# Attention with a gMLP behind it: a fixed order in steps of two score tiles, and q and k transposed by DMA

## The chip, the cores and the metric

The kernel runs on one core of one Trainium2 chip. The metric is the device time of one launch in microseconds (us), the median of several runs; the kernels that are compared ran on the same chip in the same rounds. Most runs agree within a per cent or so; a run that is over 1.5% above the fastest of its kernel counts as slow and stays out of the ratios.

The engines go by the profiler's names: PE is TensorE (matmuls), ACT is ScalarE, DVE VectorE, POOL GpSimd, and SP SyncE, which issues DMA transfers. An eviction is the copy or operation that takes a result out of PSUM, where PE writes it, into SBUF. The granted clock is the share of its full clock that PE was given.

## The reference

For 8 batches, 12 heads, 448 positions and a head width of 64: q and k are normalized by their root mean square, attention follows, and its output goes through a gMLP (two matmuls with a spatial mixing between them).

```python
def rmsnorm(x, g):
    rms = np.sqrt(np.mean(x * x, axis=-1, keepdims=True) + 1e-06)
    return x / rms * g
q_n, k_n = (rmsnorm(q, g_q), rmsnorm(k, g_k))
scores = scale * np.matmul(q_n, k_n.transpose(0, 1, 3, 2))
attn = softmax(scores); x = attn @ v        # cut: written out in the original
h = np.maximum(x @ w_in, 0.0)               # [8, 448, 1024]
u, v = h[..., :512], h[..., 512:]
v_n = (v - mu) / np.sqrt(var + 1e-06)       # layer norm over the 512
v_s = np.einsum('ts,bsd->btd', w_spatial, v_n) + b_spatial[None, :, None]
return (u * v_s) @ w_out                    # [8, 448, 768]
```

The results are compared with this reference; every kernel in this document was correct.

## The kernel before

Work goes in groups of four heads, three groups to a batch, 24 in all. One group has eight score tiles (112x896 each), so a batch has 24 exps of 896 columns. A scheduler orders the instructions; the gMLP of a finished batch is doled out between the exps by a table of costs.

```python
ps_sc = ctx.enter_context(tc.tile_pool(name="ps_sc", bufs=2, space=PSUM))
qn_pool = ctx.enter_context(tc.tile_pool(name="qn", bufs=2))
...
def transposes(G, pr):                      # 8 PE transposes, two evictions by DVE
    ps = ps_w.tile([128, 8, 128], BF, name="ps")
    for i in range(2):
        for c in range(NC):
            pe.matmul(out=ps[:, 4 * i + c, 0:P],
                      lhsT=nrm[G, i][:, c, 2 * pr:2 * pr + 2, :],
                      rhs=ident[0:P, 0:P], is_transpose=True, ...)
    dve.tensor_copy(out=t[:, 0], in_=ps[:, 0:4, 0:P])
    dve.tensor_scalar(out=t[:, 1], in0=ps[:, 4:8, 0:P], scalar1=g2_col, ...)
...
def expo(G, n):                             # one tile: 2 banks, 896 columns
    act.activation(out=exps[G, pr][:, c, :, :], in_=sct[G, n][:, :, 0:S], func=AF.Exp, ...)
...
for st in range(NST + 4):                   # 96 steps of two exps
    expo(G, 2 * n); expo(G, 2 * n + 1)
    # cut: loads, squares, scaling, transposes of later groups
    while work and debt > 0:                # gMLP units, by their cost
        cost, fn = work.popleft(); debt -= cost; fn()
    scores(G1, 2 * n1); scores(G1, 2 * n1 + 1)
```

Of the kernel before, what the change touches and what calls it, by code (L numbers as in the profile page):

```python
# [19 lines left out]
def kernel(  # L20
# [17 lines left out]
    P = 112  # L38
# [6 lines left out]
    act.preload_act_table_set("natural_log_exp_and_others")  # L45

    const = ctx.enter_context(tc.tile_pool(name="const", bufs=1))
    ps_sc = ctx.enter_context(tc.tile_pool(name="ps_sc", bufs=2, space=PSUM))
# [4 lines left out]
    qt_pool = ctx.enter_context(tc.tile_pool(name="qt", bufs=2))  # L53
    st_pool = ctx.enter_context(tc.tile_pool(name="st", bufs=3))
# [12 lines left out]
    def load_qk(G):  # L67
        b, g = divmod(G, NG)
        qf = qk_pool.tile([P, 4, NC * D], FP, name="qf")
        kf = qk_pool.tile([P, 4, NC * D], FP, name="kf")  # L70
        for l in (0, 2) if G == 0 else (0,):
            r = slice(l, l + 2) if G == 0 else slice(0, 4)
            sync.dma_start(out=qf[:, r], in_=q_g[b][g][:, r])
            sync.dma_start(out=kf[:, r], in_=k_g[b][g][:, r])
        raw[G] = (qf, kf)

    def load_v(b):
# [6 lines left out]
    gq_col = const.tile([128, 1], FP)  # L84
    gk_col = const.tile([128, 1], FP)
    g2_col = const.tile([128, 1], FP)
    act.dma_start(out=gq_col, in_=bass.AP(tensor=g_q.tensor, offset=g_q.offset, ap=[[0, 2], [1, D]]))
    act.dma_start(out=gk_col, in_=bass.AP(tensor=g_k.tensor, offset=g_k.offset, ap=[[0, 2], [1, D]]))
    load_qk(0)
    load_qk(1)  # L90


    eps = const.tile([128, 1], FP)
    dve.memset(eps, 1e-6)
    ones = const.tile([P, 32], BF)
# [3 lines left out]

    dve.scalar_tensor_tensor(out=g2_col, in0=gq_col, scalar=scale, in1=gk_col,  # L100
                             op0=ALU.mult, op1=ALU.mult)
# [5 lines left out]
    w_sp = const.tile([P, NC, S], BF)  # L107
    vn_t = [const.tile([113, NC, DH], BF, name=f"vn{i}") for i in range(2)]

# [6 lines left out]
    def load_w_rest():  # L116
        pool.dma_start(out=w_sp, in_=moe_w_spatial.rearrange("(p c) s -> p c s", c=NC))
        pool.dma_start(out=w_out, in_=moe_w_out.rearrange("(c p) m -> p c m", p=128))
        bst = const.tile([113, S], FP)
        pool.dma_start(out=bst[96:113, :], in_=moe_b_spatial.partition_broadcast(17))  # L120
        pool.tensor_copy(out=w_spT[96:113, NC - 1, :, :],
                         in_=bst[96:113, :].rearrange("q (p c) -> q c p", c=NC))
        for t in vn_t:
            pool.memset(t[96:113, :, :], 1.0)
# [11 lines left out]
    sqs, rst, nrm, qkt = {}, {}, {}, {}  # L136

    def squares(G, i, l0=0, nl=4, eng=None):
        if G not in sqs:
            sqs[G] = st_pool.tile([P, 2, 16], FP, name="ms")  # L140
            rst[G] = st_pool.tile([P, 2, 16], FP, name="rs")
        t = sq_pool.tile([P, 4, NC * D], FP, name="sqt")
        x = raw[G][i][:, l0:l0 + nl, :]
        (eng or pool).tensor_tensor(out=t[:, 0:nl, :], in0=x, in1=x, op=ALU.mult)  # L144
        dve.tensor_reduce(out=sqs[G][:, i, NC * l0:NC * (l0 + nl)],  # L145
                          in_=t[:, 0:nl, :].rearrange("p l (c d) -> p (l c) d", d=D),
                          axis=AX.X, op=ALU.add)
# [7 lines left out]
    def scaled(G, i, l0=0, nl=4, eng=None):  # L155
        if (G, i) not in nrm:
# [3 lines left out]
            in0=raw[G][i][:, l0:l0 + nl, :].rearrange("p l (c d) -> p l c d", d=D),  # L160
            in1=rst[G][:, i, NC * l0:NC * (l0 + nl)].rearrange("p (l c) -> p l c", c=NC)
                .to_broadcast([P, nl, NC, D]),
            op=ALU.mult)

    def transposes(G, pr):
# [7 lines left out]
        t = qt_pool.tile([128, 2, NC, P], BF, name=f"qkt{pr}")  # L173
        dve.tensor_copy(out=t[:, 0], in_=ps[:, 0:4, 0:P])  # L174
        dve.tensor_scalar(out=t[:, 1], in0=ps[:, 4:8, 0:P], scalar1=g2_col, scalar2=None,
                          op0=ALU.mult)
        qkt[G, pr] = t


    exps, xts = {}, {}  # L180

    sct = {}

    def scores(G, n):
        pr, c = divmod(n, NC)
        ps = ps_sc.tile([P, 2, 512], FP, name="pss")
        t = qkt[G, pr]
        for h in range(2):
            pe.matmul(out=ps[:, h, 0:S],  # L189
                      lhsT=t[64 * h:64 * h + 64, 1, c, :],  # L190
                      rhs=t[64 * h:64 * h + 64, 0, :, :].rearrange("p c s -> p (c s)"),
                      start=True, stop=True)
        sct[G, n] = ps

    def expo(G, n):
        pr, c = divmod(n, NC)
        if c == 0:
            exps[G, pr] = e_pool.tile([P, NC, 2, S], BF, name="et")
        act.activation(out=exps[G, pr][:, c, :, :], in_=sct[G, n][:, :, 0:S],  # L199
                       func=AF.Exp, bias=0.0, scale=1.0)  # L200


    rec = {}

    def sums(G):
        ps = ps_w.tile([128, 512], FP, name="ps")
        for c in range(NC):
            for l in range(4):
                pe.matmul(out=ps[32 * l:32 * l + 32, 0:S], lhsT=ones,  # L209
                          rhs=exps[G, l // 2][:, c, l % 2, :],  # L210
                          start=(c == 0), stop=(c == NC - 1), tile_position=(0, 32 * l))
        lr = r_pool.tile([128, S], FP, name="lr")
        rc = r_pool.tile([128, S], FP, name="rc")
        act.activation(out=lr, in_=ps[:, 0:S], func=AF.Ln, bias=0.0, scale=1.0)
# [3 lines left out]
    def values(G, half):  # L218
# [4 lines left out]
        for c in range(NC):  # L223
            for l in range(4):
                pe.matmul(out=ps[32 * l:32 * l + 32, 0:S],  # L225
                          lhsT=vb[b][:, 3 * l + g, c, 32 * half:32 * half + 32],
                          rhs=exps[G, l // 2][:, c, l % 2, :],
                          start=(c == 0), stop=(c == NC - 1), tile_position=(0, 32 * l))
        dve.tensor_tensor(out=xts[b][:, 2 * g + half, :], in0=ps[:, 0:S], in1=rec[G], op=ALU.mult)  # L229


    us, vs, sts = {}, {}, {}

    def unit_v(b, c):
# [7 lines left out]
        dve.tensor_relu(out=vs[b][:, c, :], in_=ps[0:P, :])  # L242
# [4 lines left out]
    def unit_ln(b):  # L247
# [3 lines left out]
        act.activation(out=rv, in_=lv, func=AF.Exp, bias=0.0, scale=-0.5)  # L251
        for c in range(NC):
            dve.tensor_scalar(out=vn_t[b % 2][0:P, c, :], in0=vs[b][:, c, :],
                              scalar1=sts[b][:, c, 0:1], scalar2=rv[:, c:c + 1],
                              op0=ALU.subtract, op1=ALU.mult)

    def unit_u(b, f):
# [6 lines left out]
        dve.tensor_relu(out=us[b][:, f, :], in_=ps[:, 0:S])  # L264

    gts = {}
# [12 lines left out]
    osb = {}  # L279

    def unit_o(b, c, half):
        if half == 0:
            osb[b, c] = o_pool.tile([P, DM], FP, name="osb")
        ps = ps_w.tile([128, 512], FP, name="ps")
        for f in range(4):
            pe.matmul(out=ps[0:P, 0:384], lhsT=gts[b][:, f, c * P:(c + 1) * P],  # L286
                      rhs=w_out[:, f, 384 * half:384 * half + 384],
                      start=(f == 0), stop=(f == 3))
        act.activation(out=osb[b, c][:, 384 * half:384 * half + 384], in_=ps[0:P, 0:384],  # L289
                       func=AF.Copy, bias=0.0, scale=1.0)  # L290
        if half == 1:
            sync.dma_start(out=out[b].rearrange("(p c) m -> c p m", c=NC)[c], in_=osb[b, c])
# [3 lines left out]
    work = deque()  # L296

    def moe_units(b):
        for c in range(NC):
            work.append((1.35, lambda c=c: unit_v(b, c)))  # L300
        work.append((0.0, lambda: unit_ln(b)))
        for f in range(4):
            work.append((1.2, lambda f=f: unit_u(b, f)))
        for f in range(4):
            work.append((0.8, lambda f=f: unit_s(b, f)))
        for c in range(NC):
            for h in range(2):
                work.append((0.66, lambda c=c, h=h: unit_o(b, c, h)))

    for pr in range(2):  # L310
        squares(0, 0, 2 * pr, 2)
        squares(0, 1, 2 * pr, 2, dve)
        rstd(0, 2 * pr, 2)
        scaled(0, 0, 2 * pr, 2)
        scaled(0, 1, 2 * pr, 2, dve)
# [4 lines left out]
    load_qk(2)  # L320
    squares(1, 0)
    squares(1, 1, eng=dve)
    rstd(1)
    load_v(0)
    scaled(1, 0)
    scaled(1, 1, eng=dve)
    load_w_in()


    NST = NGT * 4  # L330
    FILL = 1.75
    debt = 0.0
    for st in range(NST + 4):
        G, n = divmod(st, 4)
        if st < NST:
            expo(G, 2 * n)
            expo(G, 2 * n + 1)
        if G + 3 < NGT and n == 0:
            load_qk(G + 3)
        if n == 0 and G % NG == 0 and G // NG + 1 < B:  # L340
            load_v(G // NG + 1)
        if G == 0 and n == 3:
            load_w_rest()
        if G + 2 < NGT:
            eng = dve if G < 2 else pool
            if n == 0:
                squares(G + 2, 0)
            elif n == 1:
                squares(G + 2, 1, eng=eng)
                rstd(G + 2)  # L350
            elif n == 2:
                scaled(G + 2, 0)
            else:
                scaled(G + 2, 1, eng=eng)
        if G > 0:
            if n == 0:
                sums(G - 1)
            elif n == 1:
                values(G - 1, 0)
            elif n == 2:  # L360
                values(G - 1, 1)
        if G + 1 < NGT:
            if n == 1:
                transposes(G + 1, 0)
            elif n == 3:
                transposes(G + 1, 1)
        if G == 2:
            w_sp_unit(n)
        if G > 0 and G % NG == 0 and n == 3:
            moe_units(G // NG - 1)  # L370
        debt = min(debt + FILL, FILL)
        while work and debt > 0:
            cost, fn = work.popleft()
            debt -= cost
# [37 lines left out]
```

## Time and profile before

| | before |
|---|---|
| time, median of the first 3 runs (range) | 406.47 us (404.77 to 410.65) |
| busy: PE, ACT, DVE, POOL | 79%, 56%, 56%, 47% |
| first exp; first gMLP matmul | 24.1 us; 79.1 us |
| one batch in the middle; in the last stretch | 46 to 47 us; 36.6 and 32.3 us |
| DMA queue of loads, stores (q1) | 29.7% of 16 engines over the span |

The row "one batch" is read from the timeline of PE: from the first matmul of one batch's gMLP with w_in to that of the next. The slices show where the DMA engines are full (tenths of 40 equal slices): the first eighth of the span, hardly anywhere later. What bounds the kernel, with its lines, is told at the head of the prediction.

```profile
PE   0055656986988797896798879997788999999994
DMA  9999947356348430790317821681313002200404
```

### The profile page before, as it was taken

How to read it: one execution, taken by the hardware profiler on the slowest of the kernel's cores; microseconds unless marked ns; L12 is line 12 of the kernel's file. 1: busy time of each engine (PE TensorE's matmuls, PEld its weight loads, DVE VectorE, ACT ScalarE, POOL GpSimd, SP SyncE). 2: the span in 40 equal slices, each digit the busy share in tenths (PEclk: the TensorE clock that was granted, in tenths of full speed). 3: DMA queues.
4: the chain of work that ended last, by engine and by line, in shares of the span. 5: the costliest groups of instructions: out<-in, count | busy, mean ns of one | idle time of the engine just before them, and what ended most of it. 6: DMA issues, size and time to landing. Idle time of an engine off the chain costs nothing.

```text
span 404.3 us, 6683 instructions
## 1 busy us (share of the span) xinstructions
PE 319.8 (79%) x2704; PEld 157.2 (39%) x2704; DVE 228.3 (56%) x403; ACT 227.7 (56%) x371; POOL 188.9 (47%) x114
## 2 busy tenths in 40 slices
PE   0055656986988797896798879997788999999994
PEld 0022223432454344442354334542344445444553
DVE  0365555859837566257645497266652762584290
ACT  1044563862667565863458645873549668767403
POOL 3177579897947353544636543563741233000000
PEclk9999885896999999998999998998999999999999
DMA  9999947356348430790317821681313002200404
GB/s 159 232 207 179 210 78 145 93 144 108 92 125 165 98 91 2 216 172 1 93 36 200 153 59 34 189 162 39 91 36 103 2 2 70 68 2 2 137 2 137
DMA packets 39091, 41.76 MB, mean 103 GB/s; under 512 B 1819, under 2 KB 34588, under 8 KB 39060
## 3 DMA queue, kind: packets, MB, share of 16 engines
q1 hardware_dynamic: 26400, 33.04, 29.7%
q0 software_dynamic: 12400, 8.30, 14.7%
q8 instruction: 21, 0.34, 0.4%
q14 instruction: 10, 0.08, 0.1%
q10 hardware_dynamic: 260, 0.00, 0.0%
HBM read 38.58 MB, written 11.01 MB: 123 GB/s over the span
## 4 chain that ended last, share of the span: by engine, by line
PE 31%; POOL 26%; issue 13%; DMA 13%; ACT 8%; DVE 7%; SPq 0%; POOLq 0%; DVEq 0%; ACTq 0%
POOL n L158 14%; POOL sqt L144 9%; PE ps L262 8%; DMA qf<-in_q_dram 7%; DMA kf<-in_k_dram 6%; PE ps L286 5%; ACT et L199 4%; PE pss L189 4%; PE ps L240 4%; PE ps L274 3%; PE ps L225 3%; PE ps L169 3%; DVE xt L229 2%; ACT osb L289 2%; PE ps L209 2%
## 5 line engine op out<-in xcount | busy, mean ns | idle before, releaser
L199 ACT ACTIVATE et<-pss 112x896 bf16<-112x896 f32 x192 | 166.2, 917 | 51.4 <-PE pss L189 50.8
L145 DVE TENSOR_REDUCE ms<-sqt 112x16 f32<-112x1024 f32 (+1 forms) x50 | 58.0, 1171 | 77.0 <-POOL sqt L144 76.8
L158 POOL TENSOR_TENSOR n<-qf,rs 112x1024 bf16<-112x1024 f32 (+1 forms) x25 | 50.2, 2007 | 98.4 <-PE ps L169 51.9
L189 PE MATMUL pss<-qkt 64*112 64x448 bf16 x384 | 69.5, 399 | 23.0 <-ACT et L199 20.2
L144 POOL TENSOR_TENSOR sqt<-qf 112x1024 f32<-112x1024 f32 (+1 forms) x25 | 47.1, 1883 | 39.7 <-DMA qf<-in_q_dram 36.7
L262 PE MATMUL ps<-xt,w_in 128*128 128x448 bf16 x192 | 47.3, 399 | 16.6 <-DVE xt L229 14.6
L169 PE MATMUL ps<-ident,n 112*128 112x112 bf16 x384 | 29.9, 226 | 30.4 <-POOL n L158 30.2
L225 PE MATMUL ps<-et,vt 112*32 112x448 bf16 x768 | 47.9, 364 | 3.1 <-DVE xt L229 2.9
L286 PE MATMUL ps<-w_out,gt 128*112 128x384 bf16 x256 | 48.3, 329 | 1.6 <-DVE gt L277 1.6
L189 PEld LDWEIGHTS <-qkt 64*112 64x112 bf16 x384 | 23.5, 130 | 66.2 <-issue 61.7
L152 ACT ACTIVATE lnms<-ms,eps 112x32 f32<-112x32 f32 (+1 forms) x25 | 8.0, 321 | 70.1 <-DVE ms L145 70.1
L229 DVE TENSOR_TENSOR xt<-ps,rc 128x448 bf16<-128x448 f32 x48 | 29.5, 614 | 30.9 <-PE ps L225 28.9
L240 PE MATMUL ps<-w_in,xt 128*112 128x512 bf16 x192 | 45.7, 381 | 0.1
L144 POOL TENSOR_TENSOR sqt<-kf 112x1024 f32<-112x1024 f32 x20 | 37.9, 1895 | 9.8 <-DMA kf<-in_k_dram 8.1
L169 PEld LDWEIGHTS <-n 112*128 112x128 bf16 x384 | 22.1, 104 | 48.1 <-POOL n L158 33.5
L158 POOL TENSOR_TENSOR n<-kf,rs 112x1024 bf16<-112x1024 f32 x20 | 38.2, 1912 | 0.0
L286 PEld LDWEIGHTS <-gt 128*112 128x112 bf16 x256 | 31.5, 130 | 14.2 <-DVE gt L277 3.6
L262 PEld LDWEIGHTS <-w_in 128*128 128x128 bf16 x192 | 19.6, 106 | 39.6 <-issue 27.9
L289 ACT ACTIVATE osb<-ps 112x384 f32<-112x384 f32 x64 | 29.5, 490 | 9.7 <-PE ps L286 9.5
L274 PE MATMUL ps<-w_spT,vn 112*128 112x448 bf16 (+1 forms) x128 | 29.3, 360 | 4.5 <-DVE gt L277 4.5
L240 PEld LDWEIGHTS <-xt 128*112 128x112 bf16 x192 | 22.9, 130 | 16.4 <-issue 1.9
L174 DVE COPY qkt<-ps 128x448 bf16<-128x448 bf16 x48 | 18.2, 380 | 18.6 <-PE ps L169 18.6
(38 smaller groups left out, 265.3 us busy)
## 6 DMA issues: line engine op xcount, KB each, us to landing
out_dram<-osb SPq DMA_DIRECT2D x32, 336.0 KB, 2.9
qf<-in_q_dram SPq DMA_DIRECT2D x23, 448.0 KB, 4.5
kf<-in_k_dram SPq DMA_DIRECT2D x23, 448.0 KB, 5.0
vt<-in_v_dram POOLq DMA_DIRECT2D x8, 672.0 KB, 7.6
w_in<-in_moe_w_in_dram POOLq DMA_DIRECT2D x4, 384.0 KB, 6.0
w_out<-in_moe_w_out_dram POOLq DMA_DIRECT2D x1, 768.0 KB, 12.4
qf<-in_q_dram SPq DMA_DIRECT2D x2, 224.0 KB, 4.9
kf<-in_k_dram SPq DMA_DIRECT2D x2, 224.0 KB, 6.6
```

The source lines that it names most:

```text
L144: (eng or pool).tensor_tensor(out=t[:, 0:nl, :], in0=x, in1=x, op=ALU.mult)
L145: dve.tensor_reduce(out=sqs[G][:, i, NC * l0:NC * (l0 + nl)], in_=t[:, 0:nl, :].rearrange("p l (c d) -> p (l c) d", d=D), axis=AX.X, op=AL ...
L158: (eng or pool).tensor_tensor(out=nrm[G, i][:, :, l0:l0 + nl, :].rearrange("p c l d -> p l c d"), in0=raw[G][i][:, l0:l0 + nl, :].rearrang ...
L169: pe.matmul(out=ps[:, 4 * i + c, 0:P], lhsT=nrm[G, i][:, c, 2 * pr:2 * pr + 2, :], rhs=ident[0:P, 0:P], is_transpose=True, start=(i == 0 a ...
L189: pe.matmul(out=ps[:, h, 0:S], lhsT=t[64 * h:64 * h + 64, 1, c, :], rhs=t[64 * h:64 * h + 64, 0, :, :].rearrange("p c s -> p (c s)"), star ...
L199: act.activation(out=exps[G, pr][:, c, :, :], in_=sct[G, n][:, :, 0:S], func=AF.Exp, bias=0.0, scale=1.0)
L225: pe.matmul(out=ps[32 * l:32 * l + 32, 0:S], lhsT=vb[b][:, 3 * l + g, c, 32 * half:32 * half + 32], rhs=exps[G, l // 2][:, c, l % 2, :], s ...
L229: dve.tensor_tensor(out=xts[b][:, 2 * g + half, :], in0=ps[:, 0:S], in1=rec[G], op=ALU.mult)
L240: pe.matmul(out=ps[0:P, :], lhsT=xts[b][:, j, c * P:(c + 1) * P], rhs=w_in[:, j, DH:DF], start=(j == 0), stop=(j == 5))
L262: pe.matmul(out=ps[:, 0:S], lhsT=w_in[:, j, 128 * f:128 * f + 128], rhs=xts[b][:, j, :], start=(j == 0), stop=(j == 5))
L274: pe.matmul(out=ps[:, 0:S], lhsT=vn_t[b % 2][0:kp, c, 128 * f:128 * f + 128], rhs=w_spT[0:kp, c, :, :].rearrange("p c s -> p (c s)"), star ...
L286: pe.matmul(out=ps[0:P, 0:384], lhsT=gts[b][:, f, c * P:(c + 1) * P], rhs=w_out[:, f, 384 * half:384 * half + 384], start=(f == 0), stop=( ...
```

## The change

Four things in one. (1) The scheduler gives way to a hand-written order of 99 steps, a step being two score tiles (four matmuls of 448 columns), with every gMLP unit at a fixed place. (2) The two tiles of a step share one PSUM tile of four banks; from step 12 on one exp of 1792 takes both, while the steps of the first batch are written in halves. (3) q and k of every group but the first go from SBUF to SBUF by a DMA transpose, with k scaled by g afterwards on DVE. (4) g comes as a row and gets its column form from a small matmul. Smaller parts come with the order: q and k are loaded one group further ahead, and the evictions of the gMLP are divided by hand between ACT and DVE.

```diff
-    ps_sc = ... tile_pool(name="ps_sc", bufs=2, space=PSUM)
+    ctx.enter_context(tc.manual_schedule())
+    ps_sc = ... tile_pool(name="ps_sc", bufs=1, space=PSUM)
...
+    def transpose_dma(G, i):
+        kr = qt_pool.tile([128, NC, 2, P], BF, name="kr") if i == 1 else None
+        t = qk_tiles(G)[0] if i == 0 else kr
+        sync.dma_start_transpose(out=t.rearrange("q c r p -> q (c r) p"),
+                                 in_=nrm[G, i].rearrange("p c l d -> p (c l d)"))
+    def k_scale(G):
+        dve.tensor_scalar(out=qkt[G][1], in0=krs.pop(G), scalar1=g2_col, scalar2=None, op0=ALU.mult)
+    pss = ps_sc.tile([P, 4, 512], FP, name="pss")
...
+    for t in range(NST + 3):
+        early = G < NG                      # first batch
+        if early:
+            if t > 0:
+                scores(t, 1)
+                expo(t, 0)
+            expo(t, 1)
+            scores(t + 1, 0)
+        else:
+            scores(t)                       # cut: step 12, the passage
+            expo(t)
+        if n == 1 and G % NG == 0: load_v(G // NG + 1)
+        if t == 1: load_w_in()
+        if t == 4: load_w_rest()
...
+        if n == 1: rstd(T); scaled(T, 0); scaled(T, 1); transpose_dma(T, 0); transpose_dma(T, 1)
+        if n == 0: k_scale(K)               # T = G + 2, K = G + 1
+        if moe:                             # s: step in the batch before's gMLP
+            if s == 1: stats(b, 0)
+            elif s == 2: stats(b, 1)
+            elif s == 3: stats(b, 2); stats(b, 3); ln_rstd(b)
+            elif s == 4: ln_apply(b)
-    while work and debt > 0: ...
```

## The prediction

> **What bounds the kernel now.** I read the busy shares first, then the chain that ended last, then the waits, then equal stretches of the span side by side. Busy shares and chain:
>
> ```profile
> PE 319.8 (79%) x2704; PEld 157.2 (39%) x2704; DVE 228.3 (56%) x403; ACT 227.7 (56%) x371; POOL 188.9 (47%) x114
> PE 31%; POOL 26%; issue 13%; DMA 13%; ACT 8%; DVE 7%; SPq 0%; POOLq 0%; DVEq 0%; ACTq 0%
> POOL n L158 14%; POOL sqt L144 9%; PE ps L262 8%; DMA qf<-in_q_dram 7%; DMA kf<-in_k_dram 6%; PE ps L286 5%; ACT et L199 4%; PE pss L189 4%; PE ps L240 4%; PE ps L274 3%; PE ps L225 3%; PE ps L169 3%; DVE xt L229 2%; ACT osb L289 2%; PE ps L209 2%
> ```
>
> No engine is full, and the chain is spread over PE, POOL (the squares L144 and the scaling L158) and the q and k loads: latency that goes round a ring, not a full engine. The list of waits shows the ring:
>
> ```profile
> DVE ms L145 <- POOL sqt L144: 76.8, 25, 7.4
> ACT lnms L152 <- DVE ms L145: 70.1, 20, 16.3
> POOL n L158 <- PE ps L169: 51.9, 11, 9.6
> POOL sqt L144 <- DMA qf<-in_q_dram: 36.7, 12, 5.5
> PEld L169 <- POOL n L158: 33.5, 5, 20.5
> ```
>
> A load lands, POOL squares, DVE sums, ACT makes the factor, POOL scales into n, PE transposes n; POOL waits 51.9 us for those transposes to give n back, and the next load leaves late. Windows of one batch each (12 pairs of exps; columns PE, PEld, DVE, ACT, POOL busy, clock, DMA share, GB/s), one from the middle, one from the end when POOL and the loads are nearly through:
>
> ```profile
> 143.00:190.00 47.00, 38.86 (x339) 19.15 (x338) 26.82 (x49) 27.76 (x46) 23.62 (x13) 0.97 0.43 104
> 312.20:348.70 36.50, 36.09 (x338) 17.85 (x336) 19.77 (x42) 26.94 (x41) 11.28 (x6) 1.00 0.13 39
> ```
>
> The same PE work (339 and 338 matmuls) takes 47 us in the middle and 36.5 us once the ring is gone: there PE itself is the bound. The start is separate. DVE stands 15.4 us behind a tiny load of g_k, and the DMA engines are full for the first 48 us:
>
> ```profile
> 16.32 0.16 DVE L100 SCALAR_TENSOR_TENSOR g_col<-gq_col,gk_col 128x1 f32<-128x1 f32 x1 [15.37 <-DMA gk_col<-in_g_k_dram]
> 24.00:48.00 24.00, 12.88 (x99) 5.70 (x100) 14.44 (x18) 13.65 (x22) 17.14 (x12) 0.99 1.01 192
> ```
>
> The groups from which costs come:
>
> ```profile
> L199 ACT ACTIVATE et<-pss 112x896 bf16<-112x896 f32 x192 | 166.2, 917 | 51.4 <-PE pss L189 50.8
> L169 PE MATMUL ps<-ident,n 112*128 112x112 bf16 x384 | 29.9, 226 | 30.4 <-POOL n L158 30.2
> L253 DVE TENSOR_SCALAR vn<-vs,mv,rv 112x512 bf16<-112x512 bf16 x32 | 18.2, 632 | 1.2 <-ACT rv L251 0.7
> L253 DVE TENSOR_SCALAR vn<-vs,mv,rv x32: 402/407/1996, 98.5 to 390.1; 112x512 bf16<-112x512 bf16 x32
> L145 DVE TENSOR_REDUCE ms<-sqt 112x16 f32<-112x1024 f32 x46 | 55.4, 1214 | 76.0 <-POOL sqt L144 75.9
> ```
>
> **What the Trainium skill says.** (1) "DMA: Bandwidth & Descriptors", section "Latency and other measured facts", gives 261 GB/s as an effective DMA transpose rate; nothing in this trace transposes by DMA, so it is untested here, and it is the figure I trust least. (2) "ScalarE: Activation LUTs", section "What ACT_TABLE_LOAD costs": an activation costs 186 ns plus 0.833 ns an element with immediate operands, and neighbours overlap by about 93 ns. For 896 elements that is 932 ns; the trace has 917, and pairs in 1.73 us. It agrees. (3) "SBUF — State Buffer", section "Who interferes with whom": a DVE operation in a two-port mode (a tensor_scalar from SBUF to SBUF can be one) and GpSimd lock each other out for a whole instruction. The trace agrees: L253 has a median of 407 ns and a maximum of 1996 ns, about one POOL operation more. The new scaling of k is of that kind.
>
> **The change, part by part.**
> - *Start.* g comes as one row and goes to columns by a one-column matmul, so DVE no longer stands 15.4 us. First exp at about 10 us, not 24. But the DMA engines are full, so most is not kept. Before step 15 (where the gMLP work starts) there must land q and k of six groups (6 x 0.918 = 5.5 MB), two v (1.4 MB), w_in (1.6 MB) and w_spatial (0.4 MB): 8.9 MB, at 195 GB/s 45 us; with three groups of transposes behind them I take **50 us**.
> - *Exp.* Two of 896 become one of 1792 from step 12 on. An estimate from (2): 186 + 1493 = 1.68 us alone. Two take 1.73 us now, so a bare 0.05 to 0.1 us a step, off the path once PE is the bound. But all four banks are now one buffer: scores of the next step wait for the whole exp. Loop: 1.68 + 0.58 (four score matmuls in the timeline) + about 0.2 of signals (timeline gaps of 0.1 each) = 2.46 us a step.
> - *PE transposes.* 368 of 384 leave. 8 of them take 0.57 us in the timeline, of which columns are 0.39. Per batch the columns are: scores 10752, sums 5376, values 10752, the four gMLP products 12288, 10752, 7168, 12288, transposes 5376; 74752 in all. The last batch's 24 L240 matmuls of 512 take 5.39 us, 0.439 ns a column. So 32.8 us with and **30.5 us** without the transposes: 2.54 us a step is PE's floor.
> - *PE in order.* The stretch of 36.5 us has 32.8 us of columns, so 3.7 us are waits between engines. I keep them, since the other engines get fuller: 30.5 + 3.7 = 34.2 us a batch, **2.85 us a step**.
> - *DVE.* The copies out of PSUM for q and k go (0.38 + 0.44 for each of two pairs a group: 1.64 us). One scaling of 128x896 a group comes: L253 runs 402 ns for 512, so some 0.6 us, plus now and then up to 1.9 us of POOL lock. DVE a group: reductions 2.43, scaling 1, xt 1.23, gMLP about 4.9: 9.5 of 11.4 us. ACT: 4 x 1.6 + 1.1 + 0.55 + 1.1 = 9.1 us. POOL: 4 x 1.9 = 7.7 us. All under PE, none by much.
> - *DMA transposes.* 46 of 229 KB. An estimate with (1): 0.9 us each on the engines, 5 us a batch, beside 0.43 x 47 = 20 us of present traffic: 25 of 34 us, so hidden. Latency: from the factor on ACT in step n=1 to the scaling on DVE at the next n=0 are about two steps, 5.7 us, plus the 1.2 us reduction ahead; two POOL scalings take 3.9 us and a short transpose some 3 us. It just fits.
> - *End.* Last exp to the end is 404.3 - 374.9 = 29 us, and PE is dense in it; splitting the last copies between ACT and DVE saves about one: 28 us.
>
> Sum: 50 to step 15, 81 steps x 2.85 = 231, and 28: 309 us. The hand order removes the transposes' own waits on POOL too (30 us before L169 in the whole run, partly in that stretch), which I count as 4 us: **305 us**.
>
> **Rivals.**
> - *The DMA transpose takes the place of the ring.* If small pieces make it cost 3.5 us of all engines instead of 0.9, a batch carries 20 + 21 = 41 us of DMA; 50 + 7 x 41 + 28 = 365 us. The same comes of long latency: SP issues loads, stores and transposes in one order, and DVE, in its own fixed order, would stand before the k scaling with every eviction behind it. For it: the present loads take 4.5 to 5 us to land at a share of 0.43. Against it: transposes are asked for two or three steps before need, and there is slack in SP.
> - *The single score buffer and in-order ACT become the bound.* ACT has 0.7 us a step of other work, and where it falls between exp and scores it adds: 2.46 + 0.7 = 3.2 us a step, 50 + 259 + 28 = 337 us. Against it: that work can run while PE writes scores.
> - *All fits better.* Waits halve: (30.5 + 1.9) / 12 = 2.7 us a step, and step 15 at 45 us: 45 + 219 + 27 = 291 us.
> - *Nothing gained.* A transposed load of 9 us or more would stall each group by as much as the ring now does: 390 us or above.
>
> **Range and chances.** 305 us is between the third and the main sum. The low end, 281 us, is PE at 2.6 us a step with step 15 at 43 us. The high end, 342 us, takes in the score-buffer rival and a part of the DMA one. Even the plain DMA rival at 365 us is faster by over 2%, so only the last rival makes it equal or slower. Faster 0.93, within 2% 0.03, slower 0.04.
>
> **What would show it.** Right: first exp near 10 us; only 16 of the 384 PE transposes left; a middle batch in 32 to 36 us with PE busy above 85% of it; exps of 1.65 to 1.7 us; no wait over 20 us in total of DVE on the transposed k; DMA share 0.65 to 0.8 in the middle. Wrong: DVE or PE waiting long on kr or qT, a DMA share near 1 throughout (DMA rival); ACT ending PE's idle time before the scores for over 30 us in total (score-buffer rival); POOL stretched well past 1.9 us an operation. A transpose that lands in over 6 us would make the prediction wrong.

## The result, and the profile after

| | before | after |
|---|---|---|
| time, median of 4 runs (range) | 407.08 us (404.77 to 410.65) | **355.55 us** (354.63 to 358.85) |
| first exp | 24.1 us | 12.2 us |
| first gMLP matmul (step 15 in the new order) | 79.1 us | 80.8 us |
| from there to the last batch's first gMLP matmul | 301.8 us | 247.8 us |
| from there to the end | 23.4 us | 24.2 us |

The ratio is 0.874 (0.865 to 0.883, 95%). Ratios here are the mean time of one kernel's fast runs over that of the other's of the same rounds, so not quite the ratio of the medians quoted. The prediction had the direction, but 355.55 us is outside its range of 281 to 342 us.

The table already says where the time went: all of the gain lies in the middle, and the start, for which 29 us had been expected, gained nothing. The page of the changed kernel, its busy shares, its chain, and two groups:

```profile
PE 288.7 (82%) x2338; PEld 134.5 (38%) x2338; DVE 210.6 (60%) x352; ACT 222.0 (63%) x273; POOL 186.3 (53%) x113
issue 37%; POOL 34%; PE 18%; DMA 7%; ACT 1%; DVE 1%; ACTq 0%; POOLq 0%; DVEq 0%
q1 hardware_dynamic: 69216, 43.59, 57.2%
L217 PE MATMUL pss<-qT,kT 64*112 64x448 bf16 x384 | 64.6, 408 | 39.9 <-ACT et L228 33.0
```

366 matmuls fewer show that the transposes left PE. The share of q1 rose from 29.7% of 404.3 us, 120 us, to 57.2% of 352.8 us, 202 us: the 46 transposes cost (202 - 120) / 46 = 1.8 us of all 16 engines each, twice the estimate. (Their own packets, 41216 of 256 bytes, took 78.8 us of 16 engines in this trace, 1.7 us each.) The score matmuls of the last line wait 33.0 us for exps, 20.2 before; 26 us of it fall before 80 us. One batch in the middle, and the stretch from 24 to 48 us (columns as in the prediction's windows):

```profile
188.80:224.40 35.60, 33.63 (x292) 15.65 (x288) 24.94 (x42) 26.63 (x32) 23.30 (x14) 1.00 0.83 174
24.00:48.00 24.00, 10.53 (x70) 3.75 (x69) 10.09 (x9) 11.11 (x17) 22.51 (x17) 1.00 0.96 168
```

A middle batch takes 35.6 us with PE busy for 94% of it, in place of 46 to 47. The start is the opposite: PE was busy 12.88 us of the 24 before, and is 10.53 now.

**The start.** The timeline of the changed kernel around there (start, duration, engine, line, operation; in brackets the idle time ahead and what ended it):

```profile
36.28 8.10 SPq L197 DMA_TRANSPOSE kr<-n  x1
41.41 0.62 PE L217 MATMUL pss<-qT,kT 64*112 64x448 bf16 x2 [2.31 <-ACT et L228]
43.58 0.62 PE L217 MATMUL pss<-qT,kT 64*112 64x448 bf16 x2
44.25 1.72 ACT L228 ACTIVATE et<-pss 112x896 bf16<-112x896 f32 x2 [2.41 <-PE pss L217]
46.02 0.62 PE L217 MATMUL pss<-qT,kT 64*112 64x448 bf16 x2 [1.82 <-ACT et L228]
53.57 0.45 DVE L205 TENSOR_SCALAR kT<-kr,g_col 128x896 bf16<-128x896 bf16 x1 [9.17 <-DMA kr<-n]
54.08 1.00 PE L217 MATMUL pss<-qT,kT 64*112 64x448 bf16 x4 [5.27 <-DVE kT L205]
55.11 1.72 ACT L228 ACTIVATE et<-pss 112x896 bf16<-112x896 f32 x2 [4.54 <-PE pss L217]
```

Two things are to be seen. First, PE and ACT take turns: both exps of a step run together (x2), the scores of the next half begin only when both are done, and the exps wait for the second half of the scores. The halves share one tile, and the dependence is kept for the whole tile, so they overlap no better than one buffer would. A step lasts 4.6 us (44.25 to the next exp at 48.85) although no gMLP work is in it. Second, SP stood 8.1 us in issuing a transpose whose issue takes 1.22 us in most cases, and DVE waited 9.17 us for the transposed k, which it got 17 us after that issue began (36.28 to 53.57).

PE is also slow in this part: two score matmuls take 0.62 us where four take 0.59 us later. The granted clock reads 1.00 all the same, but only because the view counts time without a clock record as full: the first record of this trace is a rise to full clock at 80.24 us. The next ones say 0.50 from 165.57 to 168.98 us, and there four score matmuls take just what four take in the start:

```profile
71.20 0.99 PE L217 MATMUL pss<-qT,kT 64*112 64x448 bf16 x4 [1.82 <-ACT et L228]
165.72 0.99 PE L217 MATMUL pss<-qT,kT 64*112 64x448 bf16 x4
```

So the matmul times say that PE ran at half its clock until about 80 us. In e1 and e9 below, the first record comes at 38.9 and 38.1 us. What the slow PE added to the start is not shown by any run; at the later pace (0.35 us for two) the scores of a step would take some 0.5 us less of its 4.6, an estimate.

**The middle.** One view gathers what has to do with the transposed k (tile kr):

```profile
L205 DVE TENSOR_SCALAR kT<-kr,g_col x23: 436/445/1837, 31.1 to 301.2; 128x896 bf16<-128x896 bf16 x23
  DMA kr<-n: 18.0, 8
DMA to landing us min/median/max: 2.9/3.6/7.6
```

DVE waited 18.0 us for it, in 8 of 23 groups; of these some 7 us fall in the middle, about once a batch. (The landing line leaves out the transpose of 36.28 us, whose landing isn't recorded.) The record shows which ones are late: all five long landings of k after 100 us, 6.0 to 7.6 us, follow the load of a later batch's v, 672 KB issued 8 us earlier and taking 13 us to land. No run moved these loads, so that they are the cause is not shown. What a late k leads to is seen in the batch shown above, from 198 us on:

```profile
198.17 0.45 DVE L205 TENSOR_SCALAR kT<-kr,g_col 128x896 bf16<-128x896 bf16 x1 [1.19 <-DMA kr<-n]
203.38 0.18 DVE L290 BATCH_NORM_AGGREGATE mv<-s 112x2 f32<-112x6 f32 x1
203.60 0.30 ACT L297 ACTIVATE lv<-mv,eps 112x4 f32<-112x4 f32 x1 [2.37 <-DVE mv L290]
204.46 1.66 ACT L228 ACTIVATE et<-pss 112x1792 bf16<-112x1792 f32 x1
206.17 0.59 PE L217 MATMUL pss<-qT,kT 64*112 64x448 bf16 x4 [1.64 <-ACT et L228]
```

DVE, in its fixed order, is late with the layer norm's statistics; ACT, in its own fixed order, waits 2.37 us for them ahead of an exp, and PE 1.64 us for the score tile. Over the run the layer norm's operation on ACT (L297) waited 16.0 us in 8 times, once a batch.

In one batch (152.4 to 190.6 us, 38.2 us long) it is worse. Windows of 2 us:

```profile
162.00:164.00 2.00, 0.23 (x8) 0.10 (x1) 1.97 (x4) 1.06 (x1) 2.00 (x2) 1.00 1.05 261
164.00:166.00 2.00, 1.55 (x8) 0.75 (x9) 1.97 (x5) 0.00 (x0) 2.00 (x2) 0.89 1.27 145
166.00:168.00 2.00, 2.00 (x8) 0.59 (x5) 1.93 (x6) 0.02 (x1) 2.00 (x2) 0.50 0.91 181
168.00:170.00 2.00, 2.00 (x9) 0.85 (x7) 2.00 (x4) 1.97 (x4) 0.46 (x1) 0.75 0.88 271
```

and its timeline:

```profile
160.85 1.90 POOL L168 TENSOR_TENSOR n<-qf,rs 112x1024 bf16<-112x1024 f32 x1 [3.77 <-ACT rs L163]
161.16 1.84 DVE L205 TENSOR_SCALAR kT<-kr,g_col 128x896 bf16<-128x896 bf16 x1 [2.36 <-DMA kr<-n]
164.45 0.73 PE L312 MATMUL ps<-xt,w_in 128*128 128x448 bf16 x3 [2.22 <-DVE vs L275]
```

The transposed k came 2.36 us late, just after POOL had begun; the scaling took 1.84 us in place of 0.45 and ended a quarter of a microsecond after POOL's operation did. PE then stood 2.22 us for an eviction by DVE, and the granted clock was 0.50 from 165.57 to 168.98 us.

### The profile page after: what moved, and what is told of

It is laid out like the page before. It is cut to its first block, busy times and chain, and to the rows that moved or that the text cites. A ratio compares the mean times of both kernels' runs of the same rounds, so it can differ in the third digit from the quotient of the medians.

```text
span 352.8 us, 5856 instructions
## 1 busy us (share of the span) xinstructions
PE 288.7 (82%) x2338; PEld 134.5 (38%) x2338; DVE 210.6 (60%) x352; ACT 222.0 (63%) x273; POOL 186.3 (53%) x113
## 3 DMA queue, kind: packets, MB, share of 16 engines
q1 hardware_dynamic: 69216, 43.59, 57.2%
## 4 chain that ended last, share of the span: by engine, by line
issue 37%; POOL 34%; PE 18%; DMA 7%; ACT 1%; DVE 1%; ACTq 0%; POOLq 0%; DVEq 0%
POOL sqt L148 19%; POOL n L168 12%; PE ps L336 5%; DMA qT<-n 4%; PE ps L283 4%; PE ps L312 3%; PE pss L217 2%; PE ps L257 2%; PE ps L322 2%; POOL vt L74 2%; ACT et L228 1%; DMA out_dram<-osb 1%; DMA g_row<-in_g_k_dram 1%; PE ps L238 1%; POOL w_in L121 1%
## 5 line engine op out<-in xcount | busy, mean ns | idle before, releaser
L228 ACT ACTIVATE et<-pss 112x1792 bf16<-112x1792 f32 (+1 forms) x109 | 160.4, 1483 | 68.8 <-PE pss L217 67.9
L217 PE MATMUL pss<-qT,kT 64*112 64x448 bf16 x384 | 64.6, 408 | 39.9 <-ACT et L228 33.0
L265 DVE TENSOR_TENSOR xt<-ps,rc 128x448 bf16<-128x448 f32 x48 | 29.6, 617 | 41.2 <-PE ps L257 35.7
L217 PEld LDWEIGHTS <-kT 64*112 64x112 bf16 x384 | 22.1, 134 | 79.2 <-issue 66.8
L148 POOL TENSOR_TENSOR sqt<-qf 112x1024 f32<-112x1024 f32 x23 | 44.4, 1932 | 0.0
L312 PE MATMUL ps<-xt,w_in 128*128 128x448 bf16 x192 | 41.3, 361 | 2.2 <-DVE vs L275 2.2
L336 PEld LDWEIGHTS <-gt 128*112 128x112 bf16 x256 | 31.3, 129 | 18.4 <-issue 11.1
L283 PEld LDWEIGHTS <-xt 128*112 128x112 bf16 x192 | 23.4, 130 | 19.4 <-issue 6.6
L341 DVE COPY osb<-ps 112x384 f32<-112x384 f32 x46 | 24.4, 553 | 7.5 <-PE ps L336 5.9
L257 PEld LDWEIGHTS <-vt 112*32 112x32 bf16 x768 | 16.8, 100 | 26.4 <-issue 19.5
L312 PEld LDWEIGHTS <-w_in 128*128 128x128 bf16 x192 | 17.6, 100 | 24.2 <-issue 11.1
L238 PE MATMUL ps<-et,ones 112*32 112x448 bf16 x384 | 24.8, 382 | 0.0
L325 DVE TENSOR_TENSOR gt<-ps,us 128x448 bf16<-128x448 f32 x32 | 20.0, 625 | 6.8 <-PE ps L322 4.5
L289 DVE BATCH_NORM_STATS2 s<-vs 112x6 f32<-112x512 bf16 x32 | 21.8, 680 | 2.5 <-ACT vs L273 2.5
```

The lines of the kernel that those rows point to most:

```text
L148: (eng or pool).tensor_tensor(out=t[:, 0:nl, :], in0=x, in1=x, op=ALU.mult)
L217: pe.matmul(out=pss[:, 2 * c + h, 0:S], lhsT=kT[64 * h:64 * h + 64, c0 + c, pr, :], rhs=qT[64 * h:64 * h + 64, :, pr, :], start=True, stop ...
L228: act.activation(out=exps[G, pr][:, 2 * c0 + a:2 * c0 + a + m, :], in_=pss[:, a:a + m, 0:S], func=AF.Exp, bias=0.0, scale=1.0)
L238: pe.matmul(out=ps[32 * l:32 * l + 32, 0:S], lhsT=ones, rhs=exps[G, l // 2][:, 2 * c + l % 2, :], start=(c == 0), stop=(c == NC - 1), tile ...
L257: pe.matmul(out=ps[32 * l:32 * l + 32, 0:S], lhsT=vb[b][:, 3 * l + g, c, 32 * half:32 * half + 32], rhs=exps[G, l // 2][:, 2 * c + l % 2, ...
L265: dve.tensor_tensor(out=xts[b][:, 2 * g + half, :], in0=pst.pop((G, half))[:, 0:S], in1=rec[G], op=ALU.mult)
```

## The experiments

All ran with three rounds (the last three with five) beside the kernel before. All outputs are right. "First gMLP" is the time of the first w_in matmul; "batches" are the distances from one batch's to the next, in the profiled run.

| run | what | median us | ratio | first gMLP | batches |
|---|---|---|---|---|---|
| (after) | the change | 355.55 | 0.874 | 80.8 | 36.1 35.5 38.2 35.6 35.6 35.5 31.3 |
| e1 | whole steps from step 1 | 349.10 | 0.856 | 73.7 | 36.1 35.7 36.4 37.9 35.3 35.1 31.3 |
| e2 | two score tiles | 349.76 | 0.858 | 72.6 | 37.1 35.6 38.0 37.1 35.1 35.4 31.3 |
| e3 | layer norm's factor one step later | 347.09 | 0.854 | 79.4 | 36.8 33.9 36.2 34.3 33.9 33.9 31.3 |
| e4 | PE transposes in the new order | 364.46 | 0.895 | 81.7 | 40.0 37.0 37.0 37.0 37.0 37.0 32.1 |
| e5 | e1 and e3 | 340.06 | 0.835 | 73.6 | 36.1 33.9 36.2 34.1 33.9 33.9 31.3 |
| e6 | e1, weights loaded later | 352.17 | 0.869 | 67.5 | 44.1 35.2 38.2 35.6 35.1 35.2 31.3 |
| e7 | weights later alone | 354.66 | 0.870 | 77.6 | 39.8 35.3 38.2 35.4 35.4 35.8 31.3 |
| e8 | e1, e3, weights later | 342.54 | 0.841 | 66.9 | 42.8 33.9 37.7 33.9 33.9 33.9 31.3 |
| e9 | e5, groups 1 to 4 on PE | 330.67 | 0.810 | 64.3 | 36.8 33.9 34.1 33.9 37.7 33.9 31.3 |
| e10 | e5, groups 1 and 2 on PE | 336.16 | 0.824 | 64.5 | 36.7 36.2 37.7 33.9 33.9 37.7 31.3 |
| e11 | e5, a third transpose a group | 341.81 | 0.832 | (slow) | (slow) |
| e12 | e9, k scaled three steps later | 367.61 | 0.907 | 63.8 | 41.6 40.3 40.3 41.9 40.3 41.8 31.3 |
| e14 | e9, k scaled on ACT | 329.96 | 0.815 | 63.3 | 36.6 34.4 34.4 34.4 34.9 34.4 31.3 |
| e15 | the change, k scaled on ACT | 346.82 | 0.855 | 80.6 | 36.7 34.4 34.4 34.4 34.4 34.4 31.3 |

The theory after reading the traces: the start is lost to the shared score tile (theory A), the middle's excess to the wait for the layer norm. The rival for the start is theory B: transposes stand behind other loads in full DMA queues.

**e1: whole steps.**

```diff
-        early = G < NG
+        early = t < 1            # cut: step 12, too, takes the later form
```

> Edit: steps 1 to 12 no longer split into halves; they take the later form (four score matmuls, then one exp of 1792). The changed kernel reached the first gMLP step at 80 us, where 50 us was predicted; its steps 4 to 11 took 4.65 us each. Theory A (one score tile makes both halves wait for both exps, so PE and ACT take turns: 1.72 exps + 0.62 + 1.69 + 0.62 us): whole steps run exp beside the sums and values, as steps 12 to 14 did at 2.75 us; eight steps save up to 1.9 us each, 15 us, so about 340 us, with L283 starting near 65 us. Theory B (the start is bound by loads and by transposes queued behind them): nothing or little is won, 350 to 356 us, and the stalls on kr and on squares grow by what the steps give.

It measured 349.10 us, and the first gMLP step came 7 us earlier. Steps now take some 2.75 us, as theory A has it. But then:

```profile
36.42 9.07 SPq L197 DMA_TRANSPOSE kr<-n  x1
53.84 0.45 DVE L205 TENSOR_SCALAR kT<-kr,g_col 128x896 bf16<-128x896 bf16 x1 [13.27 <-DMA kr<-n]
55.38 1.66 ACT L228 ACTIVATE et<-pss 112x1792 bf16<-112x1792 f32 x1 [10.48 <-PE pss L217]
```

With the alternation gone, the same late transpose shows as one stall of 10 us. So theory A holds for the length of a step, and B takes half of what A would have given, 7 us in place of 15. (Part of the 7 us may be the clock, whose first record is at 38.9 us here.)

**e2: two score tiles of two banks**, with exps of 896 throughout.

```diff
-    pss = ps_sc.tile([P, 4, 512], FP, name="pss")
+    pss2 = [ps_sc.tile([P, 2, 512], FP, name=f"pss{i}") for i in range(2)]
...
-                pe.matmul(out=pss[:, 2 * c + h, 0:S],
+                pe.matmul(out=pss2[c][:, h, 0:S],
```

> Edit: the four banks of scores are two tiles of two banks, and every exp is 896 wide again; order unchanged. Theory A: in steps 1 to 12 the halves no longer wait for each other, so a step falls from 4.65 us to about 3.2 us and the start is shorter by about 10 us; in the middle two exps cost 0.05 to 0.1 us more a step, but scores of a half need only its own exp, so the middle stays within 2 us a batch of 35.6. In all 340 to 352 us. Theory B: the start stays at 80 us and the total at 355 us or a little above.

The start gains 8 us from the other side: the halves were a good idea, and only the common tile undid it. The middle stays where it was (35.1 to 38.0 us), so one score buffer is not what bounds it. That takes the prediction's second rival off the middle.

**e3: the layer norm's factor one step later**, behind that step's exp.

```diff
                 stats(b, 3)
-                ln_rstd(b)
             elif s == 4:
+                ln_rstd(b)
                 ln_apply(b)
```

> Edit: the two small activations of the layer norm factor (L297, L298) move from gMLP step 3 to step 4, behind that step's exp. In the changed kernel ACT stood 2 to 2.5 us a batch before L297 for the statistics of DVE, with the next exp behind it, and that step took 4.6 us instead of 2.9. If the excess of the middle over my 34.2 us a batch is this wait: 33 to 34.5 us a batch, seven batches, so 341 to 348 us. If PE has its own reasons (its columns are 30.5 us of 35.6): no change, 353 to 357 us.

347.09 us. Four of six middle batches take 33.9 to 34.3 us, which is the prediction's 34.2. The start did not move. So ACT's wait for the statistics was the middle's excess; why the statistics were late is a question for e15.

**e4: the transposes back on PE**, in the new order, with DVE's two evictions and none of the DMA transposes.

```diff
-            transpose_dma(T, 0)
-            transpose_dma(T, 1)
-        if n == 0 and 3 <= K < NGT:
-            k_scale(K)
+        if n == 3 and 3 <= T < NGT:
+            transposes(T, 0)
+        if n == 0 and 3 <= K < NGT:
+            transposes(K, 1)
```

> Edit: the DMA transposes of groups 1 to 23 are undone: PE transposes into PSUM with the two DVE copies, in the same hand-written order (first half at the end of step n=3, second at the end of the next n=0). It tells what the DMA transposes alone are worth. If they give what I counted (PE columns 2.3 us a batch, 0.57 us for eight): 2.3 to 3.4 us a batch longer, 38 to 39 us a batch, 375 to 380 us. If they cost as much by their load on the DMA engines (1.8 us of all engines each by the trace, not 0.9) and the stall on kr at 44 to 54 us, the start is shorter by some 8 us and the total is 360 to 370 us. If the hand order alone carries the gain, 350 to 358 us.

364.46 us: of the change's 52 us, all but the DMA transposes carries about 43, and the DMA transposes 9. The ring at the head of the prediction, POOL waiting for PE's transposes, is gone from this run's list of waits too, so the order broke it and not the DMA. It is a steady kernel, five batches at 37.0 us. PE is busy for some 36.0 us of such a batch, and 33.6 in the changed kernel (its middle batch above): the 2.4 us between them are what the prediction counted for the transposes' columns. q1 takes 34.5% of 362.3 us, 125 us, which puts a DMA transpose at (202 - 125) / 46 = 1.7 us of all engines by a second way.

**e5: e1 and e3 together.**

> Whole steps from step 1 on (as in e1) and the layer norm's rstd at the fourth gMLP step behind that step's exp (as in e3). Theory: the two are separate costs, one of the start-up (7 us) and one of every middle batch (8 us), and add: 339 to 342 us, first gMLP step at 73 to 75 us, middle periods 33.9 us. Rival: they share a wait (the same transposes or the same DMA load limits both), and the sum stays near 346.

340.06 us, inside the expectation: the two losses are separate and add. A middle batch of it:

```profile
213.80:247.70 33.90, 33.60 (x291) 15.59 (x290) 24.67 (x42) 26.82 (x31) 23.35 (x14) 1.00 0.93 183
```

PE is busy for 33.60 us of 33.90, so nothing but PE itself bounds such a batch.

**e6, e7 and e8: the loads of w_in, the second v and the other weights later**, on e1, on the changed kernel and on e5.

```diff
-        if n == 1 and G % NG == 0 and G // NG + 1 < B:
+        if (t == 8 if G < NG else n == 1 and G % NG == 0) and G // NG + 1 < B:
             load_v(G // NG + 1)
-        if t == 1:
+        if t == 6:
             load_w_in()
-        if t == 4:
+        if t == 10:
             load_w_rest()
```

> Whole steps from step 1 on (as in e1), and the loads of w_in, the second v and the other weights issued later (steps 6, 8 and 10 in place of 1, 1 and 4). Theory B, that the transposes of the second and third group stand behind these loads: the stall of some 10 us between 43 and 55 us goes, the first gMLP step comes at 62 to 66 us, total 338 to 342. Rival: the DMA rings are full all through the start-up, so the stall only moves: first gMLP step at 71 us or later, total 346 to 350.

> The changed kernel with only the loads moved as in e6. Theory A, that the alternating halves of PE and ACT set the pace of steps 4 to 11: the wait for the transposes is mostly hidden behind them, total 350 to 355, first gMLP step at 76 to 80 us. Rival, theory B alone: the loads are the whole loss, total 341 to 345 and first gMLP step near 66 us.

> Whole steps, layer norm later and loads later, all three. If all add: 329 to 334 us, first gMLP step at 62 to 66 us, middle periods 33.9 us. If the loads only move the stall: 338 to 342.

In e6 and e8 the first gMLP step comes at 67 us, but a stall of 11.0 and 10.3 us then stands in the next batch, before the exps at 79.7 and 78.0 us; e7 gains nothing that can be told. None gives time: the stall only moved, as the rival for e6 had it. It is again a late k: in e6 DVE waits 10.17 us for one until 73.95 us. The DMA share there is 0.52 from 24 to 48 us, in place of 0.97 in e1, but SP stands 8.0 us in issuing a transpose at 66.6 us, while w_out (issued at 57.4 us, 14.7 us to landing) and a v (at 62.5 us, 17.2 us) are on their way. By these traces the stall comes where transposes meet big loads, and the position of the loads decides where that is.

**e9 and e10: groups 1 to 4, or 1 and 2, on PE; the later groups by DMA.**

```diff
-            transpose_dma(T, 0)
-            transpose_dma(T, 1)
+            if T > 4:
+                transpose_dma(T, 0)
+                transpose_dma(T, 1)
...
+        if n == 3 and 3 <= T <= 4:
+            transposes(T, 0)
+        if n == 0 and 3 <= K <= 4:
+            transposes(K, 1)
```

> The version of e5 (whole steps, layer norm later), with groups 1 to 4, those that the start-up needs, transposed on PE as before and only the later ones by DMA. Theory C, that the start-up is bound by its DMA work (0.9 of 16 engines busy from 2 us to 78 us) and the transposes there are 14 us too much of it: the stall of 10 us at 44 us goes, first gMLP step at 60 to 64 us (14 steps of 2.75 us after the exp at 23 us), total 327 to 332. Rival: the layer-norm chain of q and k (POOL and ACT) or the other loads set the pace, the stall only moves: first gMLP step at 69 us or later, total 336 to 341.

> As e9, but only groups 1 and 2 on PE, groups 3 and later by DMA. If the stall comes only from the transposes of group 2 and 3 that stood 8 and 7 us in the queue of SP, group 3's still stands in it: half of e9's gain, 332 to 337. If what counts is the sum of DMA work before 80 us, the same: half. If the first gMLP step is as early as in e9 (60 to 64 us), only the position of group 2's transposes mattered.

e9 takes 330.67 us with the first gMLP step at 64.3 us, as theory C expected. The other loads are all where they were and the DMA engines as full as ever (share 1.00 from 24 to 48 us), so the normalization of q and k and the loads do allow it; what failed was to have transposes among them. Two waits of ACT are left in e9's start:

```profile
22.55 0.32 ACT L162 ACTIVATE lnms<-ms,eps 112x32 f32<-112x32 f32 x1 [6.04 <-DVE ms L155]
31.40 0.32 ACT L162 ACTIVATE lnms<-ms,eps 112x32 f32<-112x32 f32 x1 [3.96 <-DVE ms L155]
```

L162 makes the normalization factor of the second and of the third group. In ACT's fixed order it stands ahead of the exps of the second and the fourth step (at 23.04 and 31.89 us), whose scores are ready before; no run moved it. e10's start is as early, 64.5 us, so the two groups that met the fullest queue were enough; a bound by the sum of DMA work would have left half of the loss, as its expectation has it, since half of these transposes are still there. That e10 is still 5.5 us slower than e9 lies in its middle: three batches have the pattern of a late k, PE idle for 2.22 us each time, where e9 has one. In two of the three the granted clock then fell to 0.50 for 3.4 us, and these batches take 37.7 us; in the third it stayed at 1.00, and the batch takes 36.2. It fell in e9's one (37.7 us) and not in those of e3 and e5 (36.2 us). So the idle time costs 2.2 us, the fall some 1.5 us more, and the same idle time does not always bring it.

**e11: a third DMA transpose a group from group 6 on**, q once more into a tile that nothing reads.

> The version of e5 with a third DMA transpose per group (q once more, into a spare tile that nothing reads) from group 6 on, 18 in all, some 1.7 us of all 16 engines each, 31 us of added DMA work, beside some 250 us. If the transposes of the middle are hidden (DMA share 0.63 to 0.94 there), the middle batches stay at 34 to 35 us and the total at 340 to 346. If they are not (rival 1 of the prediction: the DMA takes the place of the old bound), each batch gains up to 4 x 1.7 = 7 us on a part of them: 355 to 370.

The median is 341.81 us, two of the four runs are slow by the rule above, and the ratios of e5 and e11 (0.835 and 0.832, fast runs alone) are not told apart. Eighteen more transposes in the middle cost nothing that shows, so the throughput of the DMA engines doesn't bound the middle. The profiled run was a slow one, so its batches are not compared.

**e12: k scaled three steps later**, on e9. The idea (theory D) was that the late k is behind the batches of 37.7 us.

```diff
-        if n == 0 and 4 < K < NGT:
+        if n == 3 and 4 < K < NGT:
             k_scale(K)
```

> The version of e9 with the scaling of k by g three steps later (fourth step of a group in place of its first; the scores that need it come in the next step). Theory D: in one batch of e9's profile (37.7 us where the others take 33.9) DVE stood 2.1 us for the transposed k, then the scaling took 2.14 us in place of 0.45 while POOL ran, PE stood 2.2 us and the granted clock read 0.5 for some 4 us; with the transposed k long landed and POOL idle none of this happens: every middle batch at 33.9 us or a little under, no scaling over 0.5 us, total 325 to 329. Rival: the scores now wait for the scaling, or it meets POOL's work in the new place too: 330 us or more.

367.61 us, a clear miss, but for a reason that the rival named. The list of waits between 82 and 290 us:

```profile
PEld L217 <- DVE kT L205: 40.2, 16, 2.7
DVE ms L155 <- POOL sqt L148: 37.4, 15, 2.9
```

In its new place the scaling stands in DVE's order behind a reduction that waits for POOL, and then meets POOL's next operation (0.93 us in place of 0.45); the scores of the next group wait 2.7 us for it. It says nothing on theory D. The same move on the changed kernel (e13) was refused before it ran: its early half scores would have read the scaled k before it was written.

**e14 and e15: k scaled on ACT, one step later**, on e9 and on the changed kernel.

```diff
-        if n == 0 and 3 <= K < NGT:
-            k_scale(K)
+        if n == 1 and 3 <= K < NGT:
+            k_scale(K, act)      # activation Copy with scale=g2_col
```

> The version of e9 with the scaling of k on ACT in place of DVE, one step later (behind that step's exp and the rstd). Theory D, as told before e12 (late transposed k, then a scaling that waits for POOL, then PE idle for 2.2 us and a granted clock of 0.5): DVE can no longer wait for a transpose, so no batch of 37.7 us is left, and the middle stays at 33.9: 325 to 329 us. The scaling costs ACT some 0.9 us a group (896 elements of a partition, as the 896 exps with 0.90). Rival: ACT in its order waits for the transpose or is too full in that step, and the exps come later: 331 us or more.

> The changed kernel with only this, the scaling of k on ACT one step later. Theory D: the batch of 38.2 us becomes 35.6 (one in the profile, so some 2 to 4 us), the start stays: 350 to 354. Rival: 355 to 357, the layer norm's wait alone sets the middle.

e15 is the telling one. It leaves the layer norm where the change put it, and yet every batch from the second to the sixth takes 34.4 us, with runs from 346.44 to 347.34 us only. Its layer norm's operation on ACT, from the view of that line (idle before it, times):

```profile
  DVE mv L293: 1.6, 3
```

16.0 us in 8 waits have become 1.6 in 3. So the statistics were late because DVE was late, and DVE was late for its k. Two things went from DVE at once, the wait for the transpose and the 0.45 us of scaling; these runs don't separate them. My expectation, 350 to 354 us, was too careful, since I had taken the layer norm's wait for a loss of its own: e3 and e15 remove the same loss at two places.

e14 takes 329.96 us. No batch of 37.7 us is left, but the scaling of 1.03 us on ACT makes each one 34.4 in place of 33.9. Against e9 that is even within the intervals (0.805 to 0.814 and 0.810 to 0.820). Both beat the changed kernel by some 25 us.

## Why the prediction was wrong

By the terms of its own sum, read in the profiled run, whose span is 352.8 us:

| term | predicted | measured |
|---|---|---|
| start to step 15 | 50 us | 80.8 us |
| 81 steps | 231 us (2.85 each) | 241.4 us (2.98 each) |
| last exp to the end | 28 us | 30.6 us |
| waits that leave PE's order | -4 us | not seen |

- **The step that failed is "with three groups of transposes behind them I take 50 us".** It was 80.8 us, which is 31 of the 48 us that are missing. I worked it out from bytes alone and took the DMA engines for the only bound. By the runs, 7 of the 31 us go with the shared score tile (e1; 8 by e2) and 9 with the transposes in full queues (e5 to e9); 14 are left in e9, from 50 to 64. Of these, 3 are the length of the steps: a first exp at 10 us and 15 steps of 2.85 us, both from the prediction, give 53. The rest lies at the head of e9's trace: the first exp came 2.4 us later than predicted, and ACT stood 6.04 and 3.96 us for the factors of coming groups, with an exp behind each. From the fourth step's exp to that of step 15 (31.9 to 63.9 us) a step takes 2.7 us. That these two waits cost their full length is read from the trace and not shown by a run.
- **The first exp** was put at 10 us and came at 12.2. Right, and worth nothing by itself, since what follows waited elsewhere.
- **The middle** was right in its floor, 34.2 us, with 33.9 to 34.4 in most middle batches of e3, e5, e9, e14 and e15; but the reading behind it was wrong. I called 3.7 us of the last stretch "waits between engines", where the line that I show has PE busy for 36.09 of 36.50 us, and PE's list of waits there has a single one, of 0.4 us. What the count of columns leaves out is inside PE's own busy time, 3.3 us then and 3.1 us in e5's batch. It happened to stay the same, so that the sum came right is partly luck. The -4 us for waits had next to nothing to take away for the same reason. The changed kernel's 35.6 us are above it because the step "it just fits" for the transposes' latency failed about once a batch. The figure there was a landing of some 3 us; the measured median of 3.6 us is near it, but in five groups it was 6.0 to 7.6 us. My own sign, "a transpose that lands in over 6 us", came true. DVE stood only 1 to 2.4 us at a time; its order passed this on to ACT, and ACT's to PE.
- **The DMA transposes.** The term of 0.9 us each was mis-sized: 1.7 to 1.8 us. The conclusion that they are hidden by throughput in the middle held all the same (e11), with a DMA share of 0.62 to 0.93 by batch in place of 0.65 to 0.8.
- **The scaling of k.** 0.6 us was predicted, 0.45 measured, and "now and then up to 1.9 us of POOL lock" is what the trace has (1.84 us). Here the page "SBUF — State Buffer", section "Who interferes with whom", and the trace agree: the scaling took 0.45 us, and 1.84 us where it met POOL. What I did not follow up was that such a delay can stop PE for 2.2 us, and that the granted clock then halves at times (e10). The exp of 1792 was estimated at 1.68 us by "ScalarE: Activation LUTs", section "What ACT_TABLE_LOAD costs"; the trace has 1.66.
- **The rivals.** The first one (DMA takes the ring's place, 365 us) was right about DVE standing before the k scaling with evictions behind it, and right only in the start about its size. The second (score buffer, 337 us) was wrong about the middle (e2) and right about the start, where I had not placed it. PE's idle time ahead of scores did exceed 30 us in total, as it said: 33.0 us, 26 of them in the start. The third (all fits better, 291 us) would have needed step 15 at 45 us, and the fourth (nothing gained) a landing of 9 us throughout; neither came.
- **The end** was 2.6 us off, which no run here takes apart.

What stays open: how much of e15's gain is the wait and how much the 0.45 us; and why the first batch takes 36 to 37 us even where the later ones take 34 (the w_spatial transposes fall into it, 2.4 us of PE, but no run took those away).

## What to carry to other kernels

Give every stage of a pipelined kernel its own floor, the start too: count its steps at the pace of the slowest engine and follow the chain to its first steps before counting bytes. In a fixed order, a DMA that is short on average but not always must not stand directly ahead of a shared in-order engine; put its consumer where slack is, or on an engine with some to spare, and look at what else that engine's order makes wait. Two halves of one tile are no double buffer where the dependence is kept for the tile.

## What the Trainium skill lacked or had wrong

- "DMA: Bandwidth & Descriptors", section "Latency and other measured facts", gives 261 GB/s as an effective rate of a DMA transpose. Here 112x1024 bf16 values (229 KB) from SBUF to SBUF took 1.7 to 1.8 us of all 16 engines, some 130 GB/s, half of it, in packets of 256 bytes.
- The same page has no figure for how long such a transpose takes to land next to other traffic: for k 2.9 us at the least, a median of 3.6 and up to 7.6 us where the landing is recorded, and 17 us for the one in the start that isn't. For its issue on SP it has sequencer cycles alone, in a table about trn3; here it was 1.22 us in most cases and up to 8.1 us while the queues were full.
- "TensorE: Matmul & The Clock Gate", Part 1 (The HAM clock gate): it says that the array falls back to half its clock after an idle window of about 3.4 us. Here the clock fell at 165.57 us though PE had been busy for 1.2 of the 3.4 us before, with 2.22 us of idle time in one piece; in e3 and e5 the same 2.22 us brought no fall.
- No page says that the clock records of a trace can start late, as they do here at 80.24 us, and that a granted clock of 1.00 in a view may then mean that nothing was recorded. The times of the matmuls tell: 0.99 us for four in the start and where the record says 0.50, 0.59 us later.
